# Attention and an MLP in one kernel: the tails of all eight batches in one pass of 512 columns, and one batch's attention half an output chunk later

## The chip, the cores and the metric

The kernel runs on one core of a Trainium2 chip. The core has a matrix engine (TensorE, PE in the profile, with PEld for its weight loads), three engines for elementwise work (VectorE or DVE, ScalarE or ACT, GpSimd or POOL), and SyncE (SP), which here only issues DMAs; POOL issues DMAs as well. Matmul results land in PSUM, everything else lives in SBUF. The metric is the device time of one execution in microseconds (us), the median of several runs.

## The reference

Two parts, one feeding the other. Attention for 8 batches, 8 heads, 576 positions and 64 values per head, without softmax: relu of q and k is scaled by a cosine and by a sine of the position, and the two halves are laid side by side (128 features).

```python
theta = np.pi / 2.0 * pos / S
def phi(x, c, s):
    r = np.maximum(x, 0.0)
    return np.concatenate([r * c, r * s], axis=-1)
q_p, k_p = phi(q, cos_w, sin_w), phi(k, cos_w, sin_w)
kv = np.einsum('bhsf,bhsd->bhfd', k_p, v)
z = np.sum(k_p, axis=2)
num = np.einsum('bhsf,bhfd->bhsd', q_p, kv)
den = np.einsum('bhsf,bhf->bhs', q_p, z)[..., None] + 1e-06
attn = num / den
```

Its result, 4608 tokens (8 batches of 576) of 512 values, goes through a two-layer MLP:

```python
h = x @ w_in                                  # 512 -> 2048
g = h * (1.0 / (1.0 + np.exp(-1.702 * h)))    # quick GELU
out = g @ w_out                               # 2048 -> 512
```

## The kernel before

**Tiling.** A batch's 576 tokens are four chunks of 128 (512 columns, `MT`) and a tail of 64. One block of the program is one batch's MLP, with the next batch's attention woven into it. `mm1(b, fc)` (L293, matmuls at L285) computes 128 of the 2048 hidden features for the 512 columns, four matmuls over the four parts of the 512 inputs; `gelu` (L288, L290) turns the PSUM result into a bf16 tile `g` on ScalarE. After 16 such steps `mm2(b, t, lo, hi)` (L330, matmuls at L335) forms output chunk t (128 tokens, 512 outputs) by 16 matmuls, and may be called in halves of 8; at the end ScalarE copies the result to `ysb` (L339) and it is stored (L342), from POOL's queue in blocks 0 to 6, from SP's in block 7.

**Tails.** The 64-token tails are handled apart. Batches 2 to 7 put their tails into one tile `xt` of 384 columns, and `mm1_tails` (L300, matmuls at L303, activation at L304) runs them together in the last block, before output chunks t = 5, 6, 7 of two tails each. Batches 0 and 1 (`TB = 2`) keep their tails in columns 512 to 575 of their own `xT` tile; `mm1_tail` (L306, matmuls at L312, activation into `gtail` at L314) runs them at the end of the first layer of blocks 0 and 1, in matmuls of 64 columns, and chunk t = 4, both tails together, is computed in block 1.

**Attention of the next batch.** The preparation: `trig_q` (L144, L155; in blocks 0 and 1's start `trig`, L135, L140 on ScalarE and L142 on VectorE) and `trig` make the relu features of q and k (`qn`, `kr`); q is transposed to `qT`, by SP's DMA from batch 2 on (`qturn_dma`, L187) and by TensorE before (`qturn_pe`, L167); `vcopy` (L157) makes v bf16 (`vt`, L163 on VectorE, L161 on ScalarE). Then `kv_mm` (L202, L207, 72 matmuls) and `kv_evac` (L210, VectorE), and for each of the five chunks c: `num_mm(c)` (L228, L232, 8 matmuls), `num_div(c)` (L236, VectorE: L240, L242, L244), and the transpose of the result into `xT` or, for the tail, `xt`: by SP's DMA (`xturn_dma`, L271, L275), or by TensorE and ScalarE for batches 0 and 1 (`xturn_mm`, L257, L262, and `xturn_evac`, L264, L269).

**What sets the order.** The order of the instructions on each engine is that of the program text (the schedule is manual); each engine runs its own list and waits for the others by semaphores. The lists around the change:
- Block 0 (L439 to L502) interleaves output chunks in quarters with batch 1's attention. POOL's queue takes the loads of batch 2 (L474 to L476) behind the reads of the old q, k and v.
- Block 1 starts inside `start_block(1)` (L357, first-layer steps 0 to 4) and goes on in the loop at L505. At step `f0` = 5 VectorE makes batch 2's q, at step 6 all nine pieces of its k and all of v (L515 to L518). Behind the first layer stand `mm1_tail` (L520), then `kv_mm`, then chunk t = 4 (L538), and then the four output chunks in halves with `num_mm` 0 to 4 between the halves (L539 to L549). Block 2's first matmul reads all 512 columns of `xT`, so it needs the transposes of chunks 0 to 3.
- SP's queue runs in order: the q transposes of the next batch, the load of the next q, the five transposes of `xturn_dma`, then the loads of k and v for the batch after (L551, L552).
- PSUM: four buffers `mm` (of 128x512 f32) are shared by the first and the second layer; two buffers `at` serve attention.

Of the kernel before, what the change touches and what calls it, by code (L numbers as in the profile page):

```python
# [9 lines left out]
F32 = mybir.dt.float32  # L10
BF16 = mybir.dt.bfloat16
AF = mybir.ActivationFunctionType
# [7 lines left out]
def kernel(  # L20
# [9 lines left out]
    nc = tc.nc  # L30
    B, H, S, D = q.shape
    d_model = H * D
    d_ff = moe_w_in.shape[1]
    KC = d_model // 128
    FC = d_ff // 128
    NS = S // 64
    MT = 512
# [4 lines left out]
    xpool = ctx.enter_context(tc.tile_pool(name="xpool", bufs=2))  # L42
    gpool = ctx.enter_context(tc.tile_pool(name="gpool", bufs=20))
    ypool = ctx.enter_context(tc.tile_pool(name="ypool", bufs=4))
    small = ctx.enter_context(tc.tile_pool(name="small", bufs=3))
    pmm = ctx.enter_context(tc.tile_pool(name="pmm", bufs=4, space=PSUM))
# [64 lines left out]
    def w_in_of(kc, fc):  # L111
        return w_in_v[fc // 4][:, kc, fc % 4, :]
# [22 lines left out]
    def trig(dst, src, j, act=False, eng=nc.vector):  # L135
        i = src[:, :, ts(j, 64)]
        for cs, w in enumerate((cosw, sinw)):
            o = dst[:, j, :, ts(cs, 64)]
            if act:
                nc.scalar.activation(o, i, AF.Relu, scale=w[:, j:j + 1])  # L140
            else:
                eng.tensor_scalar(o, i, 0.0, w[:, j:j + 1], op0=MAX, op1=MUL)  # L142
# [14 lines left out]
    def vcopy(i0, i1, act=False):  # L157
        o = vt[:, :, i0:i1, 0:64].rearrange("p j i e -> p i j e")
        i = vf[:, i0:i1].rearrange("p i (j e) -> p i j e", e=64)
        if act:  # L160
            nc.scalar.activation(o, i, AF.Copy)  # L161
        else:
            nc.vector.tensor_copy(o, i)  # L163
# [30 lines left out]
    def kv_open(i0=0, i1=NI):  # L194
        t = pat.tile([128, 2, 512], F32, name="at")
        for i in range(i0, i1):
            st["kv", i] = t[:, :, ds((i - i0) * 65, 65)]
        st["ps", i0] = t[:, :, 0:(i1 - i0) * 65]
        if i0 == 0:
            st["kvs"] = small.tile([128, 2, NI, VW], BF16, name="kvs", bufs=2)  # L200

    def kv_mm(i0, i1, rhs, col, n):  # L202
        for i in range(i0, i1):
            for j in range(NS):
                for hh in range(2):
                    r = slice(hh * 64, hh * 64 + 64)
                    nc.tensor.matmul(st["kv", i][:, hh, ds(col, n)], kr[r, j, i, :], rhs(r, i, j),  # L207
                                     start=(j == 0), stop=(j == NS - 1))

    def kv_evac(i0, i1, n=65):  # L210
        o = st["kvs"][:, :, i0:i1, 0:n]
        nc.vector.tensor_copy(o, st["ps", i0].rearrange("p hh (i e) -> p hh i e", e=65)[:, :, :, 0:n])  # L212
# [15 lines left out]
    def num_mm(c):  # L228
        ps = pat.tile([128, 2, 512], F32, name="at")
        for h in range(H):  # L230
            i, hh = divmod(h, 2)
            nc.tensor.matmul(ps[:, h // 4, ds((h % 4) * 65, 65)], qT[:, h, ts(c, 128)],  # L232
                             st["kvs"][:, hh, i, 0:65], start=True, stop=True)
        nums[c] = [ps]

    def num_div(c):  # L236
        ps = nums[c][0]
        pv = ps[:, :, 0:260].rearrange("p a (h e) -> p a h e", h=4)
        den = small.tile([128, 2, 4], F32, name="den")
        nc.vector.tensor_scalar(den, pv[:, :, :, 64], 1e-6, None, op0=ADD)  # L240
        inv = small.tile([128, 2, 4], F32, name="inv")
        nc.vector.reciprocal(inv, den)  # L242
        xn = small.tile([128, 2, 4, 64], BF16, name="xn", bufs=4)
        nc.vector.tensor_tensor(xn, pv[:, :, :, 0:64],  # L244
                                inv.unsqueeze(3).to_broadcast([128, 2, 4, 64]), op=MUL)
        nums[c].append(xn)

    x = {}

    TB = 2  # L250
    NT = (B - TB) * 64
    xt = one.tile([128, KC, NT], BF16, name="xt")

    def x_open(b):
        x[b] = xpool.tile([128, KC, S], BF16, name="xT")

    def xturn_mm(c):  # L257
        ps, xn = nums[c]
# [5 lines left out]
    def xturn_evac(b, c):  # L264
        ps = nums.pop(c)[0]
        n = 128 if c < 4 else 64
        i = ps[:, :, 264:392].bitcast(BF16).rearrange("p a (k t) -> p a k t", k=2)[:, :, :, 0:n]
        o = x[b][:, :, c * 128:c * 128 + n].rearrange("p (a k) t -> p a k t", a=2)
        nc.scalar.activation(o, i, AF.Copy)  # L269

    def xturn_dma(b, c):  # L271
        xn = nums.pop(c)[1]
        n = 128 if c < 4 else 64
        o = xt[:, :, ts(b - TB, 64)] if c == 4 and b >= TB else x[b][:, :, c * 128:c * 128 + n]
        nc.sync.dma_start_transpose(out=o, in_=xn[0:n].rearrange("p a h e -> p (a h e)"))  # L275


    gT = {}
# [15 lines left out]
        mm1_part(b, fc, 0, MT)  # L294
        gelu(fc)

    gt = {}
    gl_t = one.tile([128, FC, NT], BF16, name="gl_t")

    def mm1_tails(fc):  # L300
# [2 lines left out]
            nc.tensor.matmul(hps, w_in_of(kc, fc), xt[:, kc, :], start=(kc == 0), stop=(kc == KC - 1))  # L303
        nc.scalar.activation(gl_t[:, fc, :], hps, AF.Gelu_apprx_sigmoid)  # L304

    def mm1_tail(b, half):  # L306
        if half == 0 and b % 2 == 0:
            gt[0] = gpool.tile([128, FC, 128], BF16, name="gtail", bufs=2)
        hps = pmm.tile([128, 8, 64], F32, name="mm")
        for f in range(8):  # L310
            for kc in range(KC):
                nc.tensor.matmul(hps[:, f], w_in_of(kc, half * 8 + f), x[b][:, kc, MT:S],  # L312
                                 start=(kc == 0), stop=(kc == KC - 1))
        nc.scalar.activation(gt[0][:, ts(half, 8), ts(b % 2, 64)], hps, AF.Gelu_apprx_sigmoid)  # L314

    yp = {}
    out_j = [out[b * S:b * S + S].rearrange("(p j) d -> j p d", j=NS) for b in range(2)]

    def rows(b, t):

        if t == 4:
            return [(64 * u, 64, out_j[u][NS - 1]) for u in range(2)]
        if t > 4:
            return [(64 * u, 64, out[(w + 1) * S - 64:(w + 1) * S])
                    for u, w in enumerate((TB + 2 * (t - 5), TB + 2 * (t - 5) + 1))]
        if b < 2:
            return [(64 * u, 64, out_j[b][2 * t + u]) for u in range(2)]
        return [(0, 128, out[b * S:b * S + 512].rearrange("(p c) d -> c p d", c=4)[t])]

    def mm2(b, t, lo, hi, c0=0, c1=d_model):  # L330
        if lo == 0:
            yp[t, c0] = pmm.tile([128, d_model], F32, name="mm")
        for fc in range(lo, hi):
            w = gT[fc][:, ts(t, 128)] if t < 4 else gt[0][:, fc, :] if t == 4 else gl_t[:, fc, ts(t - 5, 128)]
            nc.tensor.matmul(yp[t, c0][:, c0:c1], w, w_out_sb[:, fc, c0:c1],  # L335
                             start=(fc == 0), stop=(fc == FC - 1))
        if hi == FC:
            ysb = ypool.tile([128, d_model], F32, name="ysb")
            nc.scalar.activation(ysb[:, c0:c1], yp[t, c0][:, c0:c1], AF.Identity)  # L339
            for p0, n, dst in rows(b, t):  # L340
                eng = nc.sync if b == B - 1 else nc.gpsimd
                eng.dma_start(out=dst[:, c0:c1], in_=ysb[p0:p0 + n, c0:c1])  # L342
# [104 lines left out]
        trig(kr, kf, j)  # L447
    for fc in range(5, FC):
        mm1(0, fc)
    mm1_tail(0, 0)  # L450
    mm1_tail(0, 1)
    for j in range(5):
        trig(qn0, qf0, j)
    for j in range(5, NS):
# [50 lines left out]
    for b in range(1, B):  # L505
        nb = b + 1 if b + 1 < B else None
        f0 = 5 if b == 1 else 0
        for fc in range(f0, FC):
            if nb is not None and fc == f0:
                for c in range(5):  # L510
                    trig_q(c)
                    qturn_dma(c)
                if nb + 1 < B:
                    load_q(nb + 1)
            if nb is not None and fc == f0 + 1:  # L515
                for j in range(NS):
                    trig(kr, kf, j)
                vcopy(0, 4)  # L518
            mm1(b, fc)
        if b < TB:  # L520
            mm1_tail(b, 0)
            mm1_tail(b, 1)
        if nb is None:
            for fc in range(FC):
                mm1_tails(fc)
            for t in (5, 6, 7):
                mm2(b, t, 0, FC)
            for t in range(3):
                mm2(b, t, 0, FC)
            mm2(b, 3, 0, FC, 0, 256)  # L530
            mm2(b, 3, 0, FC, 256, 512)
            continue
        x_open(nb)
        kv_open()
        kv_mm(0, 4, vt_rhs, 0, 65)
        kv_evac(0, 4)
        if b == 1:
            mm2(b, 4, 0, FC)  # L538
        for t in range(4):  # L539
            mm2(b, t, 0, 8)  # L540
            if t < 3:
                num_mm(2 * t)
                num_div(2 * t)
                xturn_dma(nb, 2 * t)
            mm2(b, t, 8, 16)
            if t < 2:
                num_mm(2 * t + 1)
                num_div(2 * t + 1)
                xturn_dma(nb, 2 * t + 1)  # L549
        if nb + 1 < B:  # L550
            load(kf, k, nb + 1, nc.sync)  # L551
            load(vf, v, nb + 1, nc.sync)  # L552
# [30 lines left out]
```

## Time and profile before

| | |
|---|---|
| median of 3 runs | 294.69 us (294.63 to 295.33) |
| profiled execution | 294.68 us |
| its span (first to last instruction) | 293.0 us |
| TensorE busy | 287.1 us (98% of the span) |
| VectorE, ScalarE, POOL busy | 126.5, 131.1, 38.2 us |
| first layer, 512 columns (L285) | 105.2 us in 480 matmuls |
| second layer (L335), all forms | 117.7 us with g, 10.5 us with gl_t |
| tails of batches 0 and 1 (L312) | 4.6 us in 128 matmuls |
| joint tails (L303) | 10.6 us in 64 matmuls |

A busy time counts an instruction from its start to its end, and matmuls overlap a little, so sums of busy time are slightly above the time that a piece takes in the order of the chain. The chain of waits follows the last instruction back to what released it, and gives the start and the length of each piece; DMA figures are from issue to landing.

### The profile page before, as it was taken

What the parts mean: (1) busy time and instruction counts of PE and PEld (TensorE: products, weight loads), DVE (VectorE), ACT (ScalarE), POOL (GpSimd) and SP (SyncE); (2) the same over time, 40 slices, a digit from 0 to 9 for tenths busy, and PEclk for the clock granted to TensorE, in tenths of its full rate; (3) what the DMA queues carried; (4) which work ended last, traced back from release to release, by engine and by line L of the source; (5) the groups of instructions that cost most, each with busy time, mean ns of one, the idle gap of its engine ahead of it and who ended that gap; (6) DMA issues with size and microseconds to landing.
All of it is one profiled execution on the core that took longest, in us unless ns stands there. A gap on an engine that the chain in (4) does not pass through costs nothing.

```text
span 293.0 us, 5983 instructions
## 1 busy us (share of the span) xinstructions
PE 287.1 (98%) x2433; PEld 159.3 (54%) x2433; DVE 126.5 (43%) x364; ACT 131.1 (45%) x230; POOL 38.2 (13%) x70
## 2 busy tenths in 40 slices
PE   8989999999999999999999999999999999999995
PEld 2675656857455555455545554555455545565444
DVE  4864524692263826482558156715662420000000
ACT  7947752674114631463136412641265116773111
POOL 6760031500123001100110011001100010000000
PEclk9999999999999999999999999999999999999999
DMA  7999999585268965798469946986697440000322
GB/s 250 241 220 283 376 218 355 156 161 163 56 129 288 254 185 144 239 274 216 130 206 282 250 103 191 349 191 135 154 373 93 73 117 36 3 0 6 85 91 72
DMA packets 67227, 52.36 MB, mean 179 GB/s; under 512 B 47392, under 2 KB 57376, under 8 KB 67200
## 3 DMA queue, kind: packets, MB, share of 16 engines
q1 hardware_dynamic: 59824, 32.52, 45.1%
q0 software_dynamic: 7376, 19.47, 23.4%
q8 instruction: 19, 0.31, 0.4%
q14 instruction: 8, 0.07, 0.1%
HBM read 36.70 MB, written 9.44 MB: 157 GB/s over the span
## 4 chain that ended last, share of the span: by engine, by line
PE 95%; DMA 2%; DVE 1%; ACT 0%; issue 0%; SPq 0%; ACTq 0%
PE mm L335 43%; PE mm L285 38%; PE mm L303 4%; PE at L207 3%; PE at L232 3%; DMA kf<-in_k_dram 2%; PE mm L312 1%; PE at L262 1%; PE mm L171 1%; PE at L171 1%; DVE kr L142 1%; PE mm L217 0%; PE mm L348 0%; DVE xn L244 0%; ACT xT L269 0%
## 5 line engine op out<-in xcount | busy, mean ns | idle before, releaser
L335 PE MATMUL mm<-w_out_sb,g 128*128 128x512 bf16 (+1 forms) x528 | 117.7, 373 | 0.0
L285 PE MATMUL mm<-xT,w_in 128*128 128x512 bf16 (+1 forms) x608 | 113.5, 345 | 0.0
L290 ACT ACTIVATE g<-mm 128x512 bf16<-128x512 f32 x128 | 75.6, 598 | 32.0 <-PE mm L285 31.9
L285 PEld LDWEIGHTS <-w_in 128*128 128x128 bf16 x608 | 61.9, 114 | 49.0
L335 PEld LDWEIGHTS <-g 128*128 128x128 bf16 x528 | 48.7, 98 | 49.5
L339 ACT ACTIVATE ysb<-mm 128x512 f32<-128x512 f32 (+1 forms) x37 | 21.7, 586 | 111.4 <-PE mm L335 111.4
L342 POOL DMA_DIRECT2D out_dram<-ysb x38 | 20.6, 546 | 177.4 <-ACT ysb L339 177.2
L142 DVE TENSOR_SCALAR kr<-kf,cosw 128x256 bf16<-128x256 f32 x68 | 23.7, 349 | 29.0 <-DMA kf<-in_k_dram 29.0
L244 DVE TENSOR_TENSOR xn<-at,inv 128x512 bf16<-128x512 f32 x40 | 27.6, 691 | 1.4
L142 DVE TENSOR_SCALAR kr<-kf,sinw 128x256 bf16<-128x256 f32 x68 | 23.8, 350 | 0.0
L240 DVE TENSOR_SCALAR den<-at 128x8 f32<-128x8 f32 x40 | 6.6, 166 | 37.3 <-PE at L232 37.3
L232 PEld LDWEIGHTS <-qT 128*128 128x128 bf16 x320 | 14.6, 97 | 8.3 <-issue 1.0
L212 DVE CAST kvs<-at 128x520 bf16<-128x520 f32 (+1 forms) x9 | 5.8, 639 | 30.6 <-PE at L207 30.6
L232 PE MATMUL at<-kvs,qT 128*128 128x65 bf16 x320 | 16.1, 193 | 0.8 <-ACT xT L269 0.7
L155 DVE TENSOR_SCALAR qn<-qf,sinw 128x512 bf16<-128x512 f32 (+1 forms) x30 | 14.3, 477 | 0.0
L155 DVE TENSOR_SCALAR qn<-qf,cosw 128x512 bf16<-128x512 f32 (+1 forms) x30 | 14.3, 477 | 0.0
L303 PE MATMUL mm<-xt,w_in 128*128 128x384 bf16 x64 | 10.6, 326 | 0.0
L335 PE MATMUL mm<-w_out_sb,gl_t 128*128 128x512 bf16 x48 | 10.5, 379 | 0.0
L207 PEld LDWEIGHTS <-kr 64*128 64x128 bf16 x576 | 9.2, 94 | 2.3 <-issue 2.0
L303 PEld LDWEIGHTS <-w_in 128*128 128x128 bf16 x64 | 7.2, 113 | 3.3
L304 ACT ACTIVATE gl_t<-mm 128x384 bf16<-128x384 f32 x16 | 7.8, 490 | 2.4 <-PE mm L303 2.4
L163 DVE CAST vt<-vf 128x2304 bf16<-128x2304 f32 (+1 forms) x7 | 8.9, 1265 | 0.0
(68 smaller groups left out, 125.4 us busy)
## 6 DMA issues: line engine op xcount, KB each, us to landing
kf<-in_k_dram SPq DMA_DIRECT2D x5, 1152.0 KB, 6.7
vf<-in_v_dram SPq DMA_DIRECT2D x5, 1152.0 KB, 9.8
qf<-in_q_dram SPq DMA_DIRECT2D x5, 1024.0 KB, 6.0
out_dram<-ysb POOLq DMA_DIRECT2D x20, 256.0 KB, 2.8
kf<-in_k_dram POOLq DMA_DIRECT2D x2, 1152.0 KB, 10.3
vf<-in_v_dram POOLq DMA_DIRECT2D x2, 1152.0 KB, 14.0
out_dram<-ysb POOLq DMA_DIRECT2D x18, 128.0 KB, 2.9
w_in<-in_moe_w_in_dram POOLq DMA_DIRECT2D x4, 512.0 KB, 8.8
```

Source lines behind the costliest of these rows:

```text
L142: eng.tensor_scalar(o, i, 0.0, w[:, j:j + 1], op0=MAX, op1=MUL)
L155: nc.vector.tensor_scalar(o, i, 0.0, sc, op0=MAX, op1=MUL)
L163: nc.vector.tensor_copy(o, i)
L207: nc.tensor.matmul(st["kv", i][:, hh, ds(col, n)], kr[r, j, i, :], rhs(r, i, j), start=(j == 0), stop=(j == NS - 1))
L232: nc.tensor.matmul(ps[:, h // 4, ds((h % 4) * 65, 65)], qT[:, h, ts(c, 128)], st["kvs"][:, hh, i, 0:65], start=True, stop=True)
L244: nc.vector.tensor_tensor(xn, pv[:, :, :, 0:64], inv.unsqueeze(3).to_broadcast([128, 2, 4, 64]), op=MUL)
L285: nc.tensor.matmul(hp[fc][:, t0:t1], w_in_of(kc, fc), x[b][:, kc, t0:t1], start=(kc == 0), stop=(kc == KC - 1))
L290: nc.scalar.activation(g, hp.pop(fc), AF.Gelu_apprx_sigmoid)
L303: nc.tensor.matmul(hps, w_in_of(kc, fc), xt[:, kc, :], start=(kc == 0), stop=(kc == KC - 1))
L335: nc.tensor.matmul(yp[t, c0][:, c0:c1], w, w_out_sb[:, fc, c0:c1], start=(fc == 0), stop=(fc == FC - 1))
L339: nc.scalar.activation(ysb[:, c0:c1], yp[t, c0][:, c0:c1], AF.Identity)
L342: eng.dma_start(out=dst[:, c0:c1], in_=ysb[p0:p0 + n, c0:c1])
```

## The change

Three things.

1. `xt` and `gl_t` grow from 384 to 512 columns (`NT = B * 64`), and every batch's tail goes there, `x_of(b, c)` naming the place. `mm1_tail` and `gtail` are gone; `mm1_tails` and the output chunks t = 4 to 7 in the last block cover all eight batches.
2. In block 1, `kv_mm` and `num_mm` 0 to 4 each come half an output chunk (8 matmuls of L335) later among the halves of `mm2` than in the other blocks (`lag`). In blocks 2 to 6 the new loop gives the same order as the old one.
3. In block 1, VectorE makes five of the nine pieces of batch 2's k and half of v; ScalarE makes the other four pieces, one after each of the first-layer steps 7, 9, 11 and 13, and the other half of v after step 15.

```diff
-    TB = 2
-    NT = (B - TB) * 64
+    NT = B * 64
     xt = one.tile([128, KC, NT], BF16, name="xt")
 
     def x_open(b):
-        x[b] = xpool.tile([128, KC, S], BF16, name="xT")
+        x[b] = xpool.tile([128, KC, MT], BF16, name="xT")
+
+    def x_of(b, c):
+        return xt[:, :, ts(b, 64)] if c == 4 else x[b][:, :, ts(c, 128)]
...
-        o = x[b][:, :, c * 128:c * 128 + n].rearrange("p (a k) t -> p a k t", a=2)
+        o = x_of(b, c).rearrange("p (a k) t -> p a k t", a=2)
...
-        o = xt[:, :, ts(b - TB, 64)] if c == 4 and b >= TB else x[b][:, :, c * 128:c * 128 + n]
-        nc.sync.dma_start_transpose(out=o, in_=xn[0:n].rearrange("p a h e -> p (a h e)"))
+        nc.sync.dma_start_transpose(out=x_of(b, c), in_=xn[0:n].rearrange("p a h e -> p (a h e)"))
...
-    gt = {}
...
-    def mm1_tail(b, half):
-        if half == 0 and b % 2 == 0:
-            gt[0] = gpool.tile([128, FC, 128], BF16, name="gtail", bufs=2)
-        hps = pmm.tile([128, 8, 64], F32, name="mm")
-        for f in range(8):
-            for kc in range(KC):
-                nc.tensor.matmul(hps[:, f], w_in_of(kc, half * 8 + f), x[b][:, kc, MT:S],
-                                 start=(kc == 0), stop=(kc == KC - 1))
-        nc.scalar.activation(gt[0][:, ts(half, 8), ts(b % 2, 64)], hps, AF.Gelu_apprx_sigmoid)
...
-            w = gT[fc][:, ts(t, 128)] if t < 4 else gt[0][:, fc, :] if t == 4 else gl_t[:, fc, ts(t - 5, 128)]
+            w = gT[fc][:, ts(t, 128)] if t < 4 else gl_t[:, fc, ts(t - 4, 128)]
...
-    mm1_tail(0, 0)
-    mm1_tail(0, 1)
...
-                for j in range(NS):
+                for j in range(NS if b > 1 else 5):
                     trig(kr, kf, j)
-                vcopy(0, 4)
+                vcopy(0, 4 if b > 1 else 2)
             mm1(b, fc)
-        if b < TB:
-            mm1_tail(b, 0)
-            mm1_tail(b, 1)
+            if b == 1 and fc in (7, 9, 11, 13):
+                trig(kr, kf, (fc + 3) // 2, act=True)
+        if b == 1:
+            vcopy(2, 4, act=True)
         if nb is None:
             for fc in range(FC):
                 mm1_tails(fc)
-            for t in (5, 6, 7):
+            for t in (4, 5, 6, 7):
                 mm2(b, t, 0, FC)
...
-        kv_open()
-        kv_mm(0, 4, vt_rhs, 0, 65)
-        kv_evac(0, 4)
-        if b == 1:
-            mm2(b, 4, 0, FC)
-        for t in range(4):
-            mm2(b, t, 0, 8)
-            if t < 3:
-                num_mm(2 * t)
-                num_div(2 * t)
-                xturn_dma(nb, 2 * t)
-            mm2(b, t, 8, 16)
-            if t < 2:
-                num_mm(2 * t + 1)
-                num_div(2 * t + 1)
-                xturn_dma(nb, 2 * t + 1)
+        lag = 1 if b == 1 else 0
+        for u in range(8):
+            if u == lag:
+                kv_open()
+                kv_mm(0, 4, vt_rhs, 0, 65)
+                kv_evac(0, 4)
+            if 0 <= u - lag - 1 < 5:
+                num_mm(u - lag - 1)
+                num_div(u - lag - 1)
+                xturn_dma(nb, u - lag - 1)
+            mm2(b, u // 2, 8 * (u % 2), 8 * (u % 2) + 8)
```

More of the change, by code (lines that the diff above doesn't have):

```diff
@@ L319, in rows @@
     def rows(b, t):
[L321 to L325, printed above, removed]
+        if t >= 4:
+            return [(64 * u, 64, out_j[w][NS - 1] if w < 2 else out[(w + 1) * S - 64:(w + 1) * S])
+                    for u, w in enumerate((2 * (t - 4), 2 * (t - 4) + 1))]
         if b < 2:
```

## The prediction

> **What bounds the kernel now.** I read the busy table first, then the chain that ended last, then the timelines of ScalarE, VectorE and the DMA queues around blocks 0, 1 and 2. The page, busy time of each engine and the granted clock:
>
> ```profile
> PE 287.1 (98%) x2433; PEld 159.3 (54%) x2433; DVE 126.5 (43%) x364; ACT 131.1 (45%) x230; POOL 38.2 (13%) x70
> PEclk9999999999999999999999999999999999999999
> ```
>
> TensorE is busy all the way at full clock, so only TensorE time and new holes in it count. The chain, in order of time (start us, duration us, what):
>
> ```profile
> 32.64 2.13 PE mm L312 x64
> 34.76 5.18 PE mm L335 x24
> ...
> 59.16 9.50 PE mm L285 x44
> 68.65 2.13 PE mm L312 x64
> 70.78 1.19 PE at L207 x72
> 71.97 5.29 PE mm L335 x24
> ...
> 83.16 0.24 PE at L232 x8
> 83.40 1.73 PE mm L335 x8
> 85.13 0.24 PE at L232 x8
> 85.37 5.18 PE mm L335 x24
> 90.55 13.81 PE mm L285 x64
> ...
> 255.05 10.40 PE mm L303 x64
> 265.45 24.23 PE mm L335 x128
> ```
>
> L312 is the tail pass of batches 0 and 1 (each piece 64 matmuls of 64 columns), L303 the joint tail pass (384 columns), L335 the second layer, L207/L232 attention. The pieces follow each other without a gap: from 32.64 on, every piece is TensorE work. The prices fall out: a 64-column matmul 2.13/64 = 33.2 ns, a 384-column one 10.40/64 = 162.5 ns, a 512-column one 13.81/64 = 215.8 ns.
>
> **The change part by part.**
>
> *Tails.* Gone: four calls of mm1_tail, 128 matmuls, 2.12 us (32.64 to 34.76) and 2.13 us (68.65 to 70.78): -4.25 us. Added: the 64 matmuls of mm1_tails grow from 384 to 512 columns: 64 x (215.8 - 162.5) ns = +3.41 us. The 512-column price is that of the first layer's rows, same weights, same width, contiguous operand. Moved: mm2 of the joint tail chunk of batches 0 and 1, 16 x 215.8 ns = 3.45 us, from block 1 to the last block: zero. The small width is a bad deal because a weight load of 128 columns stands before each matmul: in 32.64 to 34.76 the weight-load row is busy 2.06 of 2.12 us, against 7.21 of 10.40 in the joint pass. The Trainium skill (TensorE: Matmul & The Clock Gate, Back-to-back issue gap) gives N/2.4 + 2.5 ns for a lone gap, 29.2 ns at 64 columns, and says itself that it under-counts at small N; by it the removed passes would be worth 3.74 us and the net gain 0.33 us. The row measures these very matmuls, so it decides.
>
> *Evacuations.* Four gtail activations (0.597 us) leave ScalarE; the 16 of gl_t grow from 490 to about 598 ns (the g row, same shape) and come every 4 x 215.8 = 863 ns: hidden. Without that cover they would cost 16 x 0.11 = 1.7 us. Two 128 KB stores move from POOL's queue in block 1 to SP's in the last block, behind its first 16 matmuls of L335, some 24 us before the end, where SP only stores: nothing.
>
> *Block 0, everything 2.12 us earlier.* What must be there sooner, and is: w_out groups landed at 15.66+12.8 = 28.5, 30.9, 38.9 and 41.3 us, first used in the new frame at 32.64, 36.1, 41.3 and 46.9 (the third is the tight one, 2.4 us). The q load lands at 33.73; VectorE's share then runs to 36.4, ScalarE's eight pieces, now without the gtails ahead, to about 37.1; first transposed at 37.8 and 40.4. v landed at 36.6, its copies run at 39.4 to 41.6. POOL's queue holds batch 2's loads behind these reads; they go out about 1.4 us earlier (37.5 rather than 38.88) and landed at 46.8, 50.0 and 52.8, needed from 54.8 on. So -2.12 us is kept.
>
> *Block 1, ScalarE's share.* The tail pass also stood between block 1's first layer and batch 2's attention, as cover. New frame: VectorE starts q at 56.93 - 2.13 = 54.80, ends it at 58.8, five k pieces (10 x 0.262) at 61.4, half the v copy (0.75) at 62.1; all long before use. ScalarE takes four k pieces and half of v between the gelus. The durations are shown by block 0 (ScalarE's timeline: start, duration) and the group of L161:
>
> ```profile
> 34.80 0.60 ACT L314 ACTIVATE gtail<-mm 128x512 bf16<-128x512 f32 x1 [0.47 <-PE mm L312]
> 35.30 0.50 ACT L140 ACTIVATE qn<-qf,cosw 128x256 bf16<-128x256 f32 x1
> 35.69 0.50 ACT L140 ACTIVATE qn<-qf,sinw 128x256 bf16<-128x256 f32 x1
> 36.09 0.49 ACT L140 ACTIVATE qn<-qf,cosw 128x256 bf16<-128x256 f32 x1
> ...
> L161 ACT ACTIVATE vt<-vf 128x1152 bf16<-128x1152 f32 x1 | 1.2, 1156 | 0.0
> ```
>
> Back to back, a gelu occupies 0.50 us and a k piece 0.40. Per two output chunks that is 2 x 0.50 + 2 x 0.40 = 1.80 us against TensorE's 1.73: ScalarE falls behind by 0.43 us at the first piece, then 0.07 us a pair. Gelu 7 at 61.84 - 2.13 = 59.71; pieces and gelus then chain to gelu 15 at 66.91 (it would be ready at 66.62); v copy 67.41 to 68.57. First-layer matmuls need the gelu four chunks back, over 1.4 us of slack: hidden. TensorE: first layer ends at 66.53, half an output chunk (8 x 215.8 = 1.73) to 68.25, then L207: its k pieces are done at 66.5; its second half, which reads ScalarE's v, is the 37th matmul, at 68.25 + 36 x 16.5 ns = 68.85. Slack 0.28 us. The step from a Relu back to a gelu is in no row: 0.40 (another activation of that size follows) to 0.50 (its whole duration). I take 0.40, since all back-to-back rows overlap by 0.1; at 0.50 the copy ends 0.4 later and TensorE waits 0.15 to 0.2 us. Behind that wait stand the rest of the attention and all of mm2.
>
> *Block 1, half a chunk later.* L207 moves behind 8 matmuls, no work added. The last of the four x transposes that block 2 needs starts from num_mm(3), which ends at 83.40 before, with 90.55 - 83.40 = 7.15 us to block 2. After, 1.73 us less: 5.43 us (77.42 to 82.85). Needed: 1.23 us to its issue (84.63) and a landing of 2.4 us (chunks 0 and 2) to 3.9 us (chunk 3, as a store went out): 3.6 to 5.1 us. Hidden, by 0.3 to 1.8 us. After, the stores fall on the even chunks, so I take 2.4. On SP's queue nothing else is behind these transposes but the next loads.
>
> *Block 2.* Those loads (k and v of batch 3) follow chunk 4's transpose and so also lose 1.73 us against block 2. Before (SP's queue to landing, then VectorE):
>
> ```profile
> kf<-in_k_dram SPq DMA_DIRECT2D x1, 1152.0 KB, 7.6
> vf<-in_v_dram SPq DMA_DIRECT2D x1, 1152.0 KB, 10.3
> ...
> 95.49 0.35 DVE L142 TENSOR_SCALAR kr<-kf,cosw 128x256 bf16<-128x256 f32 x1 [5.00 <-DMA kf<-in_k_dram]
> ...
> 100.22 1.35 DVE L163 CAST vt<-vf 128x2304 bf16<-128x2304 f32 x1
> ```
>
> Preparation ended at 101.57, attention began at 104.37: 2.80 us of slack, 1.07 after. Hidden. q's transposes, behind these loads on SP, landed first at 99.9 and last near 105.8, for num_mm from 107.39, one each 1.97 us: also hidden at 1.73 less. From block 3 on all as before.
>
> **Sum:** -2.12 - 2.13 + 3.41 = -0.84 us. Profiled execution: 294.68 us (span 293.0, 1.7 around it), against the median of 294.69: the same. Forecast 293.85 us, -0.285%. With ends: 293.8 if no wait appears, 294.05 with ScalarE's wait.
>
> **The rivals.**
>
> *ScalarE late.* ScalarE holds up TensorE in L207: against it 0.28 us of slack; for it a chain with no idle time. At 0.50 us for each of the four steps and a v copy after the whole last gelu, 0.2 to 0.4 us: 294.05 to 294.25 us. The Trainium skill (ScalarE: Activation LUTs, Rules for kernel authors) says relu belongs on VectorE. The rows agree as far as they go: 0.262 us against 0.40 for the same piece, and VectorE alone would be done at 64.9, before even 66.53.
>
> *Slower: block 2's preparation.* One mechanism: k lands late, VectorE's 4.73 + 1.35 us follow, TensorE waits at L207 in block 2. It eats the gain from a landing 1.07 + 0.84 = 1.9 us later than 7.6. Where POOL issued the same size among other loads it took 9.5 and 11.1 us; at 11.1 the wait is 3.5 - 1.07 = 2.4 us: 296.3 us. Against it: SP's later k loads have a median of 6.7.
>
> *Not what it says.* The tails overlap something and give nothing, +3.41 remains: 298.1 us. The gapless chain speaks against it.
>
> *The lone-gap price.* 0.33 us gain: 294.36 us; the 2.06 of 2.12 us speaks against it.
>
> **How the numbers follow.** Forecast 0.74; ScalarE late 0.14; block 2 slower 0.07; gain absent 0.03; lone-gap price 0.02. What a measurement of this kernel can tell from no change is about 0.3%, 0.88 us (293.81 us); my sum lies 0.04 us short of that line, well inside the spread of runs of one kernel (294.63 to 295.33). So the forecast's 0.74 splits: 0.45 faster, 0.27 within, 0.02 slower (for what no view here shows). ScalarE late and the lone-gap price lie within (0.16), the other two are slower (0.10): faster 0.45, same 0.43, slower 0.12. Range: down to 293.4 (forecast, less what runs differ by), up to 294.9 (ScalarE late, and a short wait in block 2); about 0.15 lies outside.
>
> **What would show it.** No L312; L303 64 pieces in 13.8 us; block 1's L207 near 68.3 after 8 matmuls of L335; first mm2 at 32.64; block 2 at 82.85 and the joint pass at 247.35 with no gap before L207, L285 or L232. Wrong would make it: L207 of block 1 waiting for vt from L161 (ScalarE), L285 of block 2 waiting for an xT transpose, or L207 of block 2 waiting for VectorE's vt behind kf.

## The result, and the profile after

The changed kernel takes 294.15 us (median of 22 runs, 294.00 to 295.14) against 294.69 us (22 runs): ratio 0.9983, 95% interval 0.9976 to 0.9990. It is faster, by 0.54 us, about two thirds of the 0.84 us that were forecast, and within the 0.3% that the prediction drew as its line. The profiled execution took 294.13 us, its span 292.4 us.

The changed kernel's line numbers differ from L262 on: the first layer is L286 (was L285), the x transposes on SP L276 (L275), the second layer L323 (L335), the stores L330 (L342), the end of the program L560 (L578); the joint tails stay L303.

The page after, busy times and granted clock:

```profile
PE 286.3 (98%) x2305; PEld 154.7 (53%) x2305; DVE 123.9 (42%) x356; ACT 133.9 (46%) x235; POOL 37.5 (13%) x68
PEclk9999999999999999999999999999999999999999
```

The chain of work that ended last, after, in order of time (start us, duration us, what):

```profile
23.08 9.50 PE mm L286 x44
32.58 5.18 PE mm L323 x24
...
56.97 9.50 PE mm L286 x44
66.47 1.73 PE mm L323 x8
68.19 1.19 PE at L207 x72
69.38 1.83 PE mm L323 x8
...
77.12 0.24 PE at L232 x8
77.37 1.73 PE mm L323 x8
79.09 0.24 PE at L232 x8
79.34 3.45 PE mm L323 x16
82.79 13.81 PE mm L286 x64
...
247.29 13.81 PE mm L303 x64
261.10 27.68 PE mm L323 x144
288.78 0.03 ACTq L327
```

There is no tail pass; the joint pass costs 13.81 us; attention of batch 2 stands behind 8 matmuls at 68.19 without a gap before it, and block 2 starts at 82.79. Every start is 0.06 us before the one that was forecast (32.64, 68.25, 82.85, 247.35), because this execution's first piece began 0.06 us earlier. So TensorE's last piece ends at 288.78 instead of 289.68: 0.90 us, the forecast 0.84 and the 0.06 of the start. The span became only 0.54 us shorter. **The missing 0.36 us lie behind the last matmul.**

There the last store (chunk 3's second half) follows ScalarE's copy by the same steps in both kernels, and takes the same time to land. Then SP runs a list of waits at the end of the program: nine instructions, each on two semaphores (the counters by which engines and DMAs report that they are done), that stand in neither kernel's text and in the traces of both in the same order. SP's DMAs take eight semaphores in turn, and each of the eight has its place in that list. A DRAIN instruction follows, and behind it 0.85 us before and 0.83 us after pass to the end. SP's queue at the end of the kernel before, and its wait in the list for the last store:

```profile
286.88 3.61 SPq L342 DMA_DIRECT2D out_dram<-ysb  x3
...
SPq L578 <- DMA out_dram<-ysb: 1.0, 1, 1.0
```

and of the kernel after:

```profile
285.98 3.61 SPq L330 DMA_DIRECT2D out_dram<-ysb  x3
...
SPq L560 <- DMA out_dram<-ysb: 1.4, 1, 1.4
```

The wait for the last store became longer, 1.4 for 1.0 us, though the store did not: after the change SP meets it near the start of its list, stands there, and has the rest of the list still to do. The instructions of the end's line on SP's queue, between the landing of the last store and the drain that follows the list; before the change (291.97 to 292.12 us):

```profile
L578 SPq EVENT_SEMAPHORE  x2: 28/28/28, 292.0 to 292.1; - x2
L578 SPq DRAIN  x1: 13/13/13, 292.1 to 292.1; - x1
```

After the change (291.08 to 291.59 us):

```profile
L560 SPq EVENT_SEMAPHORE  x8: 28/28/28, 291.1 to 291.5; - x8
L560 SPq DRAIN  x1: 13/13/13, 291.6 to 291.6; - x1
```

Two waits end after the landing before, eight after, the last store's own counted; from landing to drain 0.144 us before, 0.511 us after. The difference, 0.37 us for six waits (0.061 each), is what is missing. What moved the place is the two stores of chunk t = 4 that came to SP's queue: the eight semaphores go round, two more DMAs (SP issues 95 before, 97 after) shift the last store from the seventh to the eighth and on to the first.

That is an argument from one pair of traces; the experiments test it, and then whether the other two parts of the change earned anything.

### The profile page after: what moved, and what is told of

Its sections match the earlier page's. It is cut to its first block, busy times and chain, and to the rows that moved or that the text cites. A ratio compares the mean times of both kernels' runs of the same rounds, so it can differ in the third digit from the quotient of the medians.

```text
span 292.4 us, 5737 instructions
## 1 busy us (share of the span) xinstructions
PE 286.3 (98%) x2305; PEld 154.7 (53%) x2305; DVE 123.9 (42%) x356; ACT 133.9 (46%) x235; POOL 37.5 (13%) x68
## 4 chain that ended last, share of the span: by engine, by line
PE 95%; DMA 2%; DVE 1%; ACT 0%; issue 0%; SPq 0%; ACTq 0%
PE mm L323 43%; PE mm L286 38%; PE mm L303 5%; PE at L207 3%; PE at L232 3%; DMA kf<-in_k_dram 2%; PE at L264 1%; PE mm L171 1%; PE at L171 1%; DVE kr L142 1%; PE mm L217 0%; PE mm L336 0%; DVE xn L244 0%; ACT xT L271 0%; SPq L62 0%
## 5 line engine op out<-in xcount | busy, mean ns | idle before, releaser
L323 PE MATMUL mm<-w_out_sb,g 128*128 128x512 bf16 (+1 forms) x528 | 117.9, 373 | 0.0
L286 PE MATMUL mm<-xT,w_in 128*128 128x512 bf16 (+1 forms) x608 | 113.5, 345 | 0.1
L286 PEld LDWEIGHTS <-w_in 128*128 128x128 bf16 x608 | 61.7, 113 | 49.1
L323 PEld LDWEIGHTS <-g 128*128 128x128 bf16 x528 | 48.7, 98 | 49.5
L330 POOL DMA_DIRECT2D out_dram<-ysb x36 | 19.4, 540 | 173.1 <-ACT ysb L327 172.7
L142 DVE TENSOR_SCALAR kr<-kf,cosw 128x256 bf16<-128x256 f32 x64 | 22.4, 350 | 28.7 <-DMA kf<-in_k_dram 28.7
L142 DVE TENSOR_SCALAR kr<-kf,sinw 128x256 bf16<-128x256 f32 x64 | 22.5, 352 | 0.0
L303 PE MATMUL mm<-xt,w_in 128*128 128x512 bf16 x64 | 14.0, 379 | 0.0
L323 PE MATMUL mm<-w_out_sb,gl_t 128*128 128x512 bf16 x64 | 14.0, 379 | 0.0
L304 ACT ACTIVATE gl_t<-mm 128x512 bf16<-128x512 f32 x16 | 9.6, 597 | 4.2 <-PE mm L303 4.2
L303 PEld LDWEIGHTS <-w_in 128*128 128x128 bf16 x64 | 7.2, 113 | 6.6
L207 PEld LDWEIGHTS <-kr 64*128 64x128 bf16 x576 | 9.2, 94 | 2.7 <-issue 2.5
L323 PEld LDWEIGHTS <-gl_t 128*128 128x128 bf16 x64 | 6.3, 98 | 7.5
```

The lines of the kernel that those rows point to most:

```text
L286: nc.tensor.matmul(hp[fc][:, t0:t1], w_in_of(kc, fc), x[b][:, kc, t0:t1], start=(kc == 0), stop=(kc == KC - 1))
```

## The experiments

Two groups, each on one chip with its own runs of the kernel before: 294.62 us (29 runs) for the first, 294.63 us (29 runs) for the second.

**1. The last store on the last of the eight semaphores.**

```diff
-                eng = nc.sync if b == B - 1 else nc.gpsimd
+                eng = nc.sync if b == B - 1 and (t, p0) != (4, 0) else nc.gpsimd
```

> The changed kernel, with one 128 KB store of the last block (first half of chunk t = 4) issued from POOL's queue instead of SP's, so that the last store of the program takes the last of the eight semaphores of SP's DMAs and not the first. Theory 'exit list': at the end SP waits for the semaphores one after the other, some 0.062 us each, and only those behind the last store's own cost time after it landed; from 7 behind it to 0 saves 7 x 0.062 = 0.43 us: 293.72 us, ratio to before 0.9967. Rival 'more stores at the end': the two stores that came to SP's queue cost 0.37 us; one fewer gives back half: 293.97 us, ratio 0.9975. Rival 'chance': no difference from the changed kernel, 294.15 us, 0.9983.

Measured: 293.73 us (7 runs), ratio 0.9972 (0.9961 to 0.9983). One wait after the landing, 0.082 us to the drain; the same line, 291.80 to 291.89 us:

```profile
L560 SPq EVENT_SEMAPHORE  x1: 28/28/28, 291.8 to 291.8; - x1
L560 SPq DRAIN  x1: 13/13/13, 291.9 to 291.9; - x1
```

One store off the queue gave back 0.43 us in the list. In the medians it gave back 0.35 us, each against the kernel before on its own chip (-0.89 for the changed kernel's -0.54). The interval of the ratio holds both the list's 0.9967 and the 0.9975 of "half of the loss", so it does not decide. Two of the seven runs (294.35 and 294.44) stand 0.6 us above the rest; the other five lie at 293.64 to 293.74, each of them below half of the loss (293.97) and below every run of the changed kernel here (294.00 and up, and 293.97 in experiment 8).

**2. The last store on the fifth.**

```diff
-                eng = nc.sync if b == B - 1 else nc.gpsimd
+                eng = nc.sync if b == B - 1 and t not in (4, 5) else nc.gpsimd
```

> The changed kernel, with four 128 KB stores of the last block (chunks t = 4 and 5) issued from POOL's queue, so that the last store takes the fifth of the eight semaphores: 3 behind it. Exit list: 4 x 0.062 = 0.25 us saved: 293.90 us, ratio 0.9973, slower than e1. More stores at the end: two fewer than before the change, all of the loss back: 293.78 us or less, ratio 0.9969, faster than e1. Chance: 294.15 us.

Measured: 293.96 us (11 runs), ratio 0.9983 (0.9974 to 0.9992). Four waits, 0.264 us, in the stretch 291.99 to 292.26 us:

```profile
L560 SPq EVENT_SEMAPHORE  x4: 28/28/28, 292.0 to 292.2; - x4
```

With three fewer stores on SP's queue than experiment 1 it is slower than that one, by 0.23 us in the medians and 0.18 us in the list. So it is not the number of stores on SP's queue. The intervals of the two ratios overlap; the order of the medians and the counted waits agree, and experiment 1's five short runs all lie below the lowest run here (293.78).

**3. The kernel before, with the change's place in the list.**

```diff
-                eng = nc.sync if b == B - 1 else nc.gpsimd
+                eng = nc.sync if b == B - 1 or (b == B - 2 and t >= 2) else nc.gpsimd
```

> The kernel before, with the last two stores of block 6 issued from SP's queue instead of POOL's, some 35 us before the end; nothing else. The last store moves from the seventh semaphore to the first. Exit list: 6 x 0.062 = 0.37 us slower, 295.06 us, ratio 1.0013. More stores at the end: these stores are long over by then, 294.69 us, ratio 1.000.

Measured: 295.02 us (11 runs), ratio 1.0015 (1.0006 to 1.0024). Eight waits, 0.511 us, in the stretch 291.93 to 292.44 us:

```profile
L578 SPq EVENT_SEMAPHORE  x8: 28/28/28, 291.9 to 292.4; - x8
```

Nothing of the change is in this kernel; its two stores were issued at 238.47 and 241.90 us, more than 51 us before the end (not the 35 us of the expectation), and it lost 0.40 us. The loss can be put on without the change and taken off with it.

**4. The joint tails alone.** No lag, and VectorE makes all of batch 2's k and v.

```diff
-                for j in range(NS if b > 1 else 5):
+                for j in range(NS):
                     trig(kr, kf, j)
-                vcopy(0, 4 if b > 1 else 2)
+                vcopy(0, 4)
             mm1(b, fc)
-            if b == 1 and fc in (7, 9, 11, 13):
-                trig(kr, kf, (fc + 3) // 2, act=True)
-        if b == 1:
-            vcopy(2, 4, act=True)
...
-        lag = 1 if b == 1 else 0
+        lag = 0
```

> The changed kernel without its second and third part: no lag of half an output chunk in block 1, all of batch 2's k and v on VectorE; only the joint tails are left. My theory: VectorE ends the preparation at about 64.7 us, before the first layer of block 1 ends at 66.47, so the two parts hide nothing and this is as fast as the changed kernel: 294.15 us, ratio 0.9983. Rival 'cover needed': attention right behind the first layer waits for the preparation or block 2 for its transposes: 0.5 us or more slower than that, 294.6 us or above, ratio 1.000 or above.

Measured: 294.00 us (11 runs), ratio 0.9979 (0.9970 to 0.9988): no slower than the whole change. From its chain and from VectorE's timeline:

```profile
56.76 9.28 PE mm L286 x43
66.05 0.15 issue
66.19 1.26 PE at L207 x72
```

```profile
63.23 1.34 DVE L163 CAST vt<-vf 128x2304 bf16<-128x2304 f32 x1
67.50 0.70 DVE L212 CAST kvs<-at 128x520 bf16<-128x520 f32 x1 [2.93 <-PE at L207]
```

VectorE ends the whole preparation at 64.57, and attention starts at 66.19: 1.6 us to spare even right behind the first layer. The 0.15 us named "issue" ahead of L207 is no loss against the changed kernel: from the first matmul of the second layer to the start of the last one it is 256.07 us here and 256.08 us there.

**5. ScalarE's share without the lag.**

```diff
-        lag = 1 if b == 1 else 0
+        lag = 0
```

> The changed kernel without the lag: attention of batch 2 right behind the first layer of block 1, ScalarE still makes four k pieces and half of v. My theory: ScalarE's v copy ends at 68.38, the 37th matmul of L207 would stand at 66.47 + 0.60 = 67.07, so TensorE waits 1.35 us there: 295.5 us, ratio 1.003. Rival 'ScalarE is never in the way' (the copy's place does not matter): 294.15 us, ratio 0.998.

Measured: 295.58 us (7 runs), ratio 1.0030 (1.0017 to 1.0042). ScalarE's timeline in block 1, and then TensorE's:

```profile
66.51 1.10 ACT L291 ACTIVATE g<-mm 128x512 bf16<-128x512 f32 x2
67.47 1.20 ACT L161 ACTIVATE vt<-vf 128x1152 bf16<-128x1152 f32 x1
...
```

```profile
66.70 0.72 PE L207 MATMUL at<-vt,kr 64*128 64x65 bf16 x36
68.72 0.72 PE L207 MATMUL at<-vt,kr 64*128 64x65 bf16 x36 [1.30 <-ACT vt L161]
```

After 36 matmuls TensorE stands for 1.30 us until ScalarE's half of v is there. That is the place that the prediction gave for its first rival; the price is higher than its 0.2 to 0.4 us, because the lag's 1.73 us are missing here. From the first matmul of the second layer to the start of the last one it is 257.55 us, 1.47 more than in the changed kernel, and the whole gain is gone.

**6. The lag without ScalarE's share.**

```diff
-                for j in range(NS if b > 1 else 5):
+                for j in range(NS):
...
-                vcopy(0, 4 if b > 1 else 2)
+                vcopy(0, 4)
...
-            if b == 1 and fc in (7, 9, 11, 13):
-                trig(kr, kf, (fc + 3) // 2, act=True)
-        if b == 1:
-            vcopy(2, 4, act=True)
```

> The changed kernel with the lag, but all of batch 2's k and v on VectorE. My theory: VectorE is done at about 64.7 us, long before 68.19: as the changed kernel, 294.15 us, ratio 0.998. Rival 'the share earns its place': slower by 0.3 us or more, 294.45 us, ratio 0.9992 or above.

Measured: 294.09 us (10 runs), ratio 0.9981 (0.9968 to 0.9994): as the changed kernel.

**7. The joint tails alone, with the store of experiment 1 on POOL's queue.** The edits of experiments 4 and 1 together.

> Joint tails alone (no lag, no ScalarE share), and one 128 KB store of the last block from POOL's queue as in the first experiment. Exit list: the full TensorE gain of 0.84 us and one wait fewer at the end than before (0.06 us): 293.75 us, ratio 0.997; the same as the first experiment. If lag or share had earned something, slower than that one.

Measured: 293.72 us (9 runs), ratio 0.9966 (0.9956 to 0.9977), the lowest of all here together with experiment 1. One wait after the landing, as in experiment 1.

**8. The changed kernel again,** on the chip of experiments 5 to 7, no edit.

> The changed kernel itself on the chip of these experiments: 0.84 us gained on TensorE, 0.37 us given back in the exit list, -0.47 us: ratio 0.9984. If the loss was chance: ratio 0.997.

Measured: 294.13 us (12 runs), ratio 0.9982 (0.9973 to 0.9991), eight waits and 0.51 us again. The loss is no chance.

The end of the program in all of them, against what the list makes of TensorE's 0.84 us. From the first matmul of the first layer to the start of the last matmul it is 272.22 us in the kernel before and 272.23 in experiment 3, and 271.37 to 271.38 in every kernel with joint tails but that of experiment 5, so the 0.84 is there in each of them:

| kernel | waits after the last landing | landing to drain, us | expected against before, us | medians against before, us |
|---|---|---|---|---|
| before | 2 | 0.144 | 0 | 0 |
| before, stores shifted (3) | 8 | 0.511 | +0.37 | +0.40 |
| changed | 8 | 0.511 | -0.47 | -0.54 |
| changed, again (8) | 8 | 0.510 | -0.47 | -0.50 |
| changed, fifth place (2) | 4 | 0.264 | -0.72 | -0.66 |
| changed, last place (1) | 1 | 0.082 | -0.90 | -0.89 |
| tails alone, last place (7) | 1 | 0.082 | -0.90 | -0.91 |
| lag without share (6) | 8 | 0.510 | -0.47 | -0.54 |
| tails alone (4) | 8 | 0.511 | -0.47 | -0.62 |
| share without lag (5) | 8 | 0.511 | +1.00 | +0.95 |

The expected column is -0.84 for TensorE where the tails are joined, plus the third column less 0.144, and plus the 1.47 us of the stall in experiment 5. It is met within 0.07 us in all rows but one: the tails alone (4) gained 0.15 us more. TensorE and the list took the same there as in the changed kernel; its profiled execution began the second layer 0.20 us earlier, and whether its other runs did is not shown. The interval of its ratio (0.9970 to 0.9988) holds the expected 0.9984. One wait costs (0.511 - 0.082)/7 = 0.061 us.

## Why the prediction was right or wrong

*Tails:* right. The two passes are gone and the joint pass costs 13.81 us, the price of the first layer's rows to the last digit; the sum on TensorE, -0.84 us, is what the chain shows from start to end. The lone-gap price (0.33 us) is refuted by that, and so is the rival in which the gain is absent.

*Evacuations and stores:* this step failed. "Two 128 KB stores move from POOL's queue ... nothing" priced them by their transfer and by the queue, both of which are indeed hidden. What was left out is that each DMA on SP's queue also advances the turn of its semaphores, and that the last store's semaphore sets how much of the end's list is behind it. Measured: +0.37 us, where the sum had nothing. The 1.7 us between span and execution, which the prediction took as fixed, did stay; it was the stretch of the span behind the last matmul that was taken as fixed and was not. The trace of before shows the list of waits and its 0.06 us steps on SP's queue; I had read the chain only to its last matmul.

*Block 0:* right; no gap. The q load landed a little later (VectorE started at 34.03 for 33.73), ScalarE ended its pieces at 37.3, POOL's loads went out at 37.62 (forecast 37.5), v's copies ran from 39.30 to 41.5.

*Block 1, ScalarE's share:* right, with the value that was taken for the step not in the trace: a Relu gives way to a gelu after 0.40 us. ScalarE's timeline of the changed kernel:

```profile
65.42 0.54 ACT L140 ACTIVATE kr<-kf,cosw 128x256 bf16<-128x256 f32 x1
65.81 0.53 ACT L140 ACTIVATE kr<-kf,sinw 128x256 bf16<-128x256 f32 x1
66.21 1.11 ACT L291 ACTIVATE g<-mm 128x512 bf16<-128x512 f32 x2
67.17 1.21 ACT L161 ACTIVATE vt<-vf 128x1152 bf16<-128x1152 f32 x1
```

The copy ended at 68.38 (forecast 68.57); TensorE needed it at 68.19 + 0.60 = 68.79. So the rival "ScalarE late" did not come, by 0.4 us where 0.28 was forecast; experiment 5 shows that the wait is real where the lag is missing, and what it costs. (At 0.50 us a step the prediction let TensorE wait 0.15 to 0.2 us; its own figures, 0.4 late against 0.28 of slack, give 0.12.) The remark that VectorE alone would be done at 64.9 was right too, and it decides what the second and third part are worth: experiments 4 and 6 do without the share and 4 without the lag as well, at no loss. The share needs the lag (5), and nothing needs the share. The Trainium skill (ScalarE: Activation LUTs, Rules for kernel authors) puts relu on VectorE. Measured here, that is neither faster nor slower while the lag stands (ratio 0.9981 in experiment 6 for 0.9983); without the lag it is faster, 294.00 us in experiment 4 for 295.58 in experiment 5.

*Half a chunk later:* right. The four transposes landed 2.4 to 3.7 us after issue, chunk 3, which block 2 waits for, in 2.4; its first matmul waited for nothing.

*Block 2:* right, with more slack than forecast, 2.0 us for 1.07: k landed in 6.7 us, not 7.6, and the preparation ended at 94.64 with attention at 96.60. The slower rival did not come.

*The numbers:* 293.85 us forecast, 294.15 measured, in the middle of 293.4 to 294.9, for a reason that none of the rivals held. That the range holds it is in part luck: its upper end was made for waits of TensorE that did not come. The figure also lies within what "ScalarE late" was to give (294.05 to 294.25), though ScalarE was not late. The chances put a little more on faster by over 0.3% than on within. Without the list's 0.37 us the sum of -0.84 would have stood 0.04 us short of that line; with the best place in the list experiments 1 and 7 came to it in the medians (-0.89 and -0.91 against 0.88), while their intervals reach to both sides of it.

## What to carry to other kernels

Where a kernel is bound by one engine without a gap, joining narrow matmuls into full-width ones can be priced from the chain, here to a hundredth of a microsecond; moving work to another place or engine, where it was already hidden, earned nothing here and made a tight spot. When an effect of a few tenths of a microsecond matters, read the trace to its last instruction: adding DMAs to SP's queue or taking them off shifted which semaphore the last one uses, even with stores more than 51 us before the end (experiment 3), and with it the end of the program, by up to 0.43 us here. That is as large as the effects one is comparing, so compare variants with the last store in the same place of the list, or move a store to another queue to put it in the best place.

## What the runs showed that I had not expected

The end of the program on SP is a serial list of nine waits, 0.061 us each, in an order that did not depend on which DMA comes last in any of the ten traces; the last store's place in it was worth 0.082 to 0.511 us from landing to drain.

A single profiled execution can be off at its start by more than this whole effect: the one of experiment 1 took 294.44 us, against the median of 293.73, since its chain began with the first q load,

```profile
1.84 6.72 DMA qf<-in_q_dram
8.59 1.14 DVE qn L142 x4
```

where before and after it was the k load, over at 6.25 and 6.20. TensorE's second layer then began 0.73 us later than in the changed kernel's execution, and the 0.43 us gained at the end could not be seen in its span (292.7 for 292.4). The stretches of the trace, not the spans, made the comparison possible.
